# Attention mask and row minimum in one VectorE instruction per score bank, in a fused attention + MoE + MoE kernel

## The chip, the cores and the metric

The kernel runs on one core of one Trainium2 chip. The metric is device time in microseconds (us), the median of three runs; lower is better. The profile is of one further execution of the same program.

## The reference

Inputs are q, k, v of shape (4 batches, 8 heads, 576 tokens, 64), a forget factor f per head and token, and the weights of two gated MoE layers (512 to 1536 and back), all in 32-bit floats. What is computed, cut to what matters:

```python
scores = scale * np.matmul(q, k.transpose(0, 1, 3, 2))        # scale = 1/8
decay  = cum[:, :, :, None] - cum[:, :, None, :]              # cum = cumsum(log(clip(f)))
scores = np.where(causal, -1000000000.0, scores + decay)      # causal: keys after the query
scores = scores - np.max(scores, axis=-1, keepdims=True)
attn = np.exp(scores)
attn = attn / (np.sum(attn, axis=-1, keepdims=True) + 1e-09)
x = np.matmul(attn, v)                                        # then tokens x 512
x = moe_ref(rms_norm(x) * g)                                  # silu(x @ wg) * (x @ wv) @ wo
return moe2_ref(x)                                            # the same without the norm
```

## The kernel before, in words

**Stages.** The 2304 tokens are cut into four groups. Groups 0 and 1 hold the first 256 tokens of two batches each, groups 2 and 3 the other 320 tokens of two batches each. For each group the attention of its 16 heads is computed, then an RMS norm, then both MoE layers. The attention of group g+1 runs beside the MoE layers of group g, which are long rows of TensorE (PE) matmuls of 128x512 (lines 1774 to 1776: three matmuls per product, since every 32-bit operand is split into a high and a low half, called `hi` and `lo`).

**The part that the diff touches** is the attention of groups 2 and 3 ("longer blocks": up to 576 keys per query), in `pair_wide` and `wide_part`. One unit is a pair of heads; there are 2 groups x 2 batches x 4 pairs = 16 units, each with three parts. Parts 0 and 1 take 128 queries each against 384 and 512 keys, one PSUM bank per head. Part 2, the joint part, takes the last 64 queries of both heads together against 576 keys, in two banks of 288 keys. For each part:

- PE computes the scores, a `hi` and a `lo` matmul per head and bank (lines 813, 814), and adds the causal mask with one more matmul of a triangular tile `mir` (line 820, 128 columns, once per bank of parts 0 and 1; line 818, 64 columns, once per joint part).
- VectorE (DVE) takes each bank's row maximum (line 831); in the joint part it merges the two banks' maxima (line 836); it multiplies by -0.125 (line 838).
- ScalarE (ACT) computes exp(0.125 x score + bias) with the sum of the row (line 849), into the SBUF tiles `dA`, `dB`, `dC` of parts 0, 1 and 2.
- DVE merges the two sums of the joint part (line 860), adds 1e-9 (line 862), takes the reciprocal (line 863); GpSimd (POOL), ACT or DVE scales the tile by it (lines 870 to 874).
- PE transposes the tile in pieces of 128x128 (line 922 in `turn`); ACT or DVE and then DVE split the result into `ph` and `pl` (lines 310, 312, 934); PE multiplies with the values (line 950).

**What sets the order.** All work is written as Python generators, and a planner (`Plan.run`) gives each engine its list of instructions while the program is built. Each step carries a cost (`pe(n)`, `dve(n)`, ...), and the planner always issues the step that can start first by these costs, with priorities among steps that start close together. Where a step may run on several engines, it picks the one that is done first. Nothing is reordered on the chip: each engine works through its list and waits on semaphores. So any change of a cost shifts the order on all engines from the first changed step on. A unit's tiles and banks come from pools (`Take`): two parts may be scored at once, and eight PSUM banks serve everything.

**The switch.** `switch` closes the tiles of the first two groups' attention and opens those of groups 2 and 3 in the same SBUF space; there POOL clears parts of the key and query tiles (lines 422 to 426), which have to wait until the old tiles' last readers are done.

Of the kernel before, what the change touches and what calls it, by code (L numbers as in the profile page):

```python
# [27 lines left out]
LOWEST = -3.0e38  # L28
# [39 lines left out]
S_PRIO = 4.25  # L68
S_AT = (60, 2)
# [165 lines left out]
def pe(n):  # L235
    return max(0.107, n / 2400 + 0.0135)


def dve(n):
    return n / 960 + 0.152  # L240
# [40 lines left out]
def tile_attention_moe_moe(  # L281
# [57 lines left out]
    mir = sb.tile([P, 4, P], F32R, name="mir")  # L339
# [16 lines left out]
    nc.vector.tensor_copy(mir[:, 3].rearrange("p (a n) -> p a n", a=2), mask[:, :D].unsqueeze(1).to_broadcast([P, 2, D]))  # L356
# [46 lines left out]
    qk_all = []  # L403

# [380 lines left out]
    def wide_part(hds, part, st, hl, ev, e0):  # L785
# [15 lines left out]
        for groups in plan_:  # L801
            bank, eb = yield Take(banks, ())

            def mm():
                for heads, k0, m, col in groups:
                    o = bank[:, col : col + m]
                    first = True
                    for x in heads:
                        k1, kb, q1, qb = hds[x].kq
                        qs = slice(320 - D * x, 448 - D * x) if joint else slice(q0, q0 + P)  # L810
                        ks = slice(k0, k0 + m)
                        last = k0 + m < kn and x == heads[-1]
                        nc.tensor.matmul(o, q1[:, qs], k1[:, ks], start=first, stop=False)  # L813
                        nc.tensor.matmul(o, qb[:, qs], kb[:, ks], start=False, stop=last)  # L814
                        first = False
                    if k0 + m == kn:
                        if joint:
                            nc.tensor.matmul(o[:, m - D :], mir[:, 3], mir[:, 1, :D], start=False, stop=True)
                        else:
                            nc.tensor.matmul(bank[:, col + kn - P : col + kn], mir[:, 0], mir[:, 1], start=False, stop=True)  # L820

            cost = sum(2 * len(h) * pe(m) for h, _, m, _ in groups) + pe(P)
# [4 lines left out]
        c = 8 * part  # L827
        for i, (bank, e) in enumerate(zip(sc, es)):
            if kind:
                m = plan_[i][0][2]  # L830
                em = yield op("DVE", dve(m), lambda: nc.vector.tensor_reduce(st[:, c + i : c + i + 1], bank[:, :m], axis=AX.X, op=ALU.max), e)  # L831
            else:
                v = bank[:, : 2 * kn].rearrange("p (a n) -> p a n", a=2)
                em = yield op("DVE", dve(2 * kn), lambda: nc.vector.tensor_reduce(st[:, c : c + 2].unsqueeze(2), v, axis=AX.X, op=ALU.max), e)
        if joint:
            em = yield op("DVE", dve(1), lambda: nc.vector.tensor_tensor(st[:, c : c + 1], st[:, c : c + 1], st[:, c + 1 : c + 2], op=ALU.max), em)
        k = 1 if joint else 2
        em = yield op("DVE", dve(k), lambda: nc.vector.tensor_scalar(st[:, c + 2 : c + 2 + k], st[:, c : c + k], -0.125, None, op0=ALU.mult), em)
        dt, e1 = yield Take(s[("dA", "dB", "dC")[part]], ())
        ex = []  # L840
        for i in range(2):
            if joint:
                o, src, b = dt[:, JOINT * i : JOINT * (i + 1)], sc[i][:, :JOINT], 0
            else:
# [5 lines left out]
                    o, src, AF.Exp, scale=0.125, bias=st[:, c + 2 + b : c + 3 + b], accum_out=st[:, c + 4 + i : c + 5 + i]  # L850
                ), em, e1,
# [6 lines left out]
        e = ex[1]  # L858
        if joint:
            e = yield op("DVE", dve(1), lambda: nc.vector.tensor_tensor(st[:, c + 4 : c + 5], st[:, c + 4 : c + 5], st[:, c + 5 : c + 6], op=ALU.add), e)  # L860
        r = st[:, c + 4 : c + 4 + k]
        e = yield op("DVE", dve(k), lambda: nc.vector.tensor_scalar(r, r, 1e-9, None, op0=ALU.add), e)
# [749 lines left out]
    def switch():  # L1612
# [10 lines left out]
        lp = late.enter_context(tc.tile_pool(name="lp", bufs=1))  # L1623
        attention_tiles(lp, 2, LATE)
# [396 lines left out]
```

## Time and profile before

| | |
|---|---|
| three runs | 1066.35, 1068.9, 1077.26 us; median 1068.9 us |
| profiled execution | 1067.34 us, of which the span from the first to the last instruction is 1065.5 us |
| granted TensorE clock | 1.00 of full speed on average |
| PE busy | 1054.7 us (99% of the span), 5585 matmuls |
| DVE busy | 781.3 us (73%) |
| ACT busy | 602.0 us (56%) |
| POOL busy | 455.7 us (43%) |
| DMA | 76.8% of the 16 DMA engines' time |

How to read it: busy time is the union of an engine's instructions. Matmuls overlap in the PE, so the duration of one (0.39 us for 512 columns) is longer than the distance from its start to the next one's start; what a matmul costs a busy PE is that distance. The attention of groups 2 and 3 lies between 304 and 763 us; from 761 us to the end PE has MoE work alone.

### The profile page before, as it was taken

What the parts mean: (1) busy time and instruction counts of PE and PEld (TensorE: products, weight loads), DVE (VectorE), ACT (ScalarE), POOL (GpSimd) and SP (SyncE); (2) the same over time, 40 slices, a digit from 0 to 9 for tenths busy, and PEclk for the clock granted to TensorE, in tenths of its full rate; (3) what the DMA queues carried; (4) which work ended last, traced back from release to release, by engine and by line L of the source; (5) the groups of instructions that cost most, each with busy time, mean ns of one, the idle gap of its engine ahead of it and who ended that gap; (6) DMA issues with size and microseconds to landing.
All of it is one profiled execution on the core that took longest, in us unless ns stands there. A gap on an engine that the chain in (4) does not pass through costs nothing. (4 is left out here: it accounts for less than half of the span.)

```text
span 1065.5 us, 17657 instructions
## 1 busy us (share of the span) xinstructions
PE 1054.7 (99%) x5585; PEld 934.9 (88%) x5585; DVE 781.3 (73%) x1632; ACT 602.0 (56%) x1322; POOL 455.7 (43%) x490
## 2 busy tenths in 40 slices
PE   8999999999999999999999999999999999999998
PEld 8988888888888888888888888888889999999998
DVE  5888888888476647666747775877877878788773
ACT  6886768775567557657326564556643325533352
POOL 1323202214367656667325675668713340244310
PEclk9999999999999999999999999999999999999999
DMA  7766798775997786775999899998895458655583
GB/s 201 226 223 227 258 354 287 244 245 172 351 371 262 254 267 207 259 269 173 344 366 368 301 341 376 363 348 292 296 365 185 170 195 257 221 185 179 190 260 103
DMA packets 136497, 281.21 MB, mean 264 GB/s; under 512 B 14674, under 2 KB 57490, under 8 KB 136402
## 3 DMA queue, kind: packets, MB, share of 16 engines
q1 hardware_dynamic: 136404, 280.09, 76.8%
q8 instruction: 44, 0.72, 0.3%
q14 instruction: 49, 0.40, 0.1%
HBM read 193.31 MB, written 86.65 MB: 263 GB/s over the span
## 5 line engine op out<-in xcount | busy, mean ns | idle before, releaser
L315 POOL TENSOR_TENSOR whl<-w,whl 128x512 fp32r<-128x512 f32 x120 | 158.0, 1324 | 191.4 <-ACT whl L310 129.6
L1774 PE MATMUL bank<-X,whl 128*128 128x512 f32 x564 | 227.7, 404 | 0.0
L1775 PE MATMUL bank<-X,whl 128*128 128x512 f32 x564 | 220.5, 391 | 0.0
L1776 PE MATMUL bank<-X,whl 128*128 128x512 f32 x564 | 220.1, 390 | 0.0
L310 ACT CAST whl<-w 128x512 fp32r<-128x512 f32 x173 | 106.0, 618 | 38.1 <-PE bank L1775 9.3
L1776 PEld LDWEIGHTS bank<-X,whl 128*128 128x128 f32 x564 | 106.0, 188 | 23.2
L1774 PEld LDWEIGHTS bank<-X,whl 128*128 128x128 f32 x564 | 106.1, 188 | 19.8
L1775 PEld LDWEIGHTS bank<-X,whl 128*128 128x128 f32 x564 | 106.2, 188 | 18.8 <-POOL X L315 0.2
L1774 PE MATMUL bank<-H,whl 128*128 128x512 f32 x211 | 84.6, 401 | 0.0
L1775 PE MATMUL bank<-H,whl 128*128 128x512 f32 x211 | 83.2, 394 | 0.0
L1776 PE MATMUL bank<-H,whl 128*128 128x512 f32 x211 | 83.0, 393 | 0.0
L1916 ACT ACTIVATE tmp<-bank 128x384 f32<-128x384 f32 x48 | 23.5, 492 | 86.8 <-DVE bank L1515 86.2
L1929 DVE SCALAR_TENSOR_TENSOR bank<-tmp,bank 128x512 f32<-128x512 f32 x60 | 41.7, 695 | 37.9 <-PE bank L1776 37.4
L1906 ACT ACTIVATE tmp<-bank 128x512 f32<-128x512 f32 x72 | 43.1, 599 | 43.2 <-PE bank L1776 42.8
L1908 DVE SCALAR_TENSOR_TENSOR tmp<-tmp,bank 128x512 f32<-128x512 f32 x72 | 49.2, 684 | 23.9 <-ACT tmp L1906 23.5
L315 DVE TENSOR_TENSOR whl<-w,whl 128x512 fp32r<-128x512 f32 x75 | 52.8, 710 | 16.9 <-ACT whl L310 16.6
L831 DVE TENSOR_REDUCE tm<-bank 128x1 f32<-128x384 f32 (+2 forms) x96 | 51.7, 561 | 8.9 <-PE bank L814 4.8
L1702 POOL TENSOR_SCALAR w<-w,rebase 128x512 f32<-128x512 f32 x22 | 18.8, 854 | 90.7 <-DMA w<-w 55.6
L934 DVE TENSOR_TENSOR pl<-bank,ph 128x512 fp32r<-128x512 f32 (+1 forms) x80 | 49.6, 631 | 7.1 <-ACT ph L310 6.4
L1719 DVE SCALAR_TENSOR_TENSOR w<-w,wk 128x512 int32<-128x512 int32 x72 | 53.7, 753 | 0.1
L1708 ACT ACTIVATE wk<-w,kbias 128x512 uint16<-128x512 uint16 x57 | 49.9, 883 | 0.4 <-DVE w L1719 0.4
L1478 PE MATMUL bank<-X,whl 128*128 128x384 f32 x150 | 50.1, 334 | 0.0
(304 smaller groups left out, 2813.7 us busy)
## 6 DMA issues: line engine op xcount, KB each, us to landing
whl<-w_split SPq DMA_DIRECT2D x89, 512.0 KB
w<-w SPq DMA_DIRECT2D x72, 512.0 KB
w<-w_f SPq DMA_DIRECT2D x144, 256.0 KB
w_split<-whl SPq DMA_DIRECT2D x72, 512.0 KB
w_f<-w SPq DMA_DIRECT2D x72, 256.0 KB
w_sums<-w SPq DMA_DIRECT2D x48, 256.0 KB
w_sums_split<-whl SPq DMA_DIRECT2D x24, 512.0 KB
w<-w_sums SPq DMA_DIRECT2D x41, 256.0 KB
```

What stands on the lines that cost most here:

```text
L310: nc.scalar.copy(o, i)
L315: (nc.vector if e == "DVE" else nc.gpsimd).tensor_tensor(o, a, b, op=ALU.subtract)
L831: em = yield op("DVE", dve(m), lambda: nc.vector.tensor_reduce(st[:, c + i : c + i + 1], bank[:, :m], axis=AX.X, op=ALU.max), e)
L934: e = yield op("DVE", dve(n), lambda: nc.vector.tensor_tensor(low, src, o.bitcast(F32), op=ALU.subtract), e)
L1478: nc.tensor.matmul(o, w[:, 0, cs], xl, start=False, stop=False)
L1708: lambda e: nc.scalar.activation(k16[:, :, 0], x16[:, :, 1], AF.Identity, scale=1.0 / 8192, bias=kbias)
L1719: lambda: nc.vector.scalar_tensor_tensor(ti, ti, 3, k, op0=ALU.logical_shift_left, op1=ALU.bitwise_or), e, et,
L1774: nc.tensor.matmul(o, wh[:, cs], xh, start=start, stop=False)
L1775: nc.tensor.matmul(o, wh[:, cs], xl, start=False, stop=False)
L1776: nc.tensor.matmul(o, wl[:, cs], xh, start=False, stop=stop)
L1906: e = yield op("ACT", actp(n), lambda: nc.scalar.activation(a, b, AF.Tanh, scale=0.5), e, e0)
L1908: "DVE", dve(n), lambda: nc.vector.scalar_tensor_tensor(a, a, 1.0, b, op0=ALU.add, op1=ALU.mult), e,
```

## The change

In `wide_part` the mask matmuls go (lines 818 and 820, and the 64-column copy of the mask in `mir`). Two SBUF tiles in the new pool hold the mask as zeros and -2^33: `whole`, 512 columns with the triangle in the last 128, and `joint`, 288 columns with a 64-column triangle at the end. In place of maximum, merge and multiplication stands one `tensor_tensor_reduce` per bank: it reads the bank and the mask, writes -0.125 x (bank + mask) back into the bank, and gives the minimum of the row. The second instruction of the joint part starts its minimum from the first one's result. The exponentials then use scale -1, and in the joint part one instruction adds both sums and 1e-9. To the planner the new instruction costs `dve(m) + TTR`, with TTR = 0.06 us. `mask_tiles` builds the two tiles at the switch, with two memsets and two selects on POOL and one small copy on DVE.

```diff
+TTR = 0.06
...
-    nc.vector.tensor_copy(mir[:, 3].rearrange("p (a n) -> p a n", a=2), mask[:, :D].unsqueeze(1).to_broadcast([P, 2, D]))
...
+    masks = {}
+
+    def mask_tiles(pool):
+        whole, joint = (pool.tile([P, n], F32, name=f"mask{n}") for n in (KN[1] - D, JOINT))
+        nc.gpsimd.memset(whole, 0.0)
+        nc.gpsimd.memset(joint, 0.0)
+        for t, rows, n in ((whole, P, P), (joint, D, D)):
+            x = t[:rows, t.shape[1] - n :]
+            nc.gpsimd.affine_select(
+                x, x, pattern=[[-1, n]], compare_op=ALU.is_ge, fill=-BIG, base=0, channel_multiplier=1
+            )
+        nc.vector.tensor_copy(joint[D:, JOINT - D :], joint[:D, JOINT - D :])
+        masks.update(whole=whole, joint=joint)
...
-                        last = k0 + m < kn and x == heads[-1]
+                        last = x == heads[-1]
...
-                    if k0 + m == kn:
-                        if joint:
-                            nc.tensor.matmul(o[:, m - D :], mir[:, 3], mir[:, 1, :D], start=False, stop=True)
-                        else:
-                            nc.tensor.matmul(bank[:, col + kn - P : col + kn], mir[:, 0], mir[:, 1], start=False, stop=True)
-
-            cost = sum(2 * len(h) * pe(m) for h, _, m, _ in groups) + pe(P)
+
+            cost = sum(2 * len(h) * pe(m) for h, _, m, _ in groups)
...
+        low, em = [], None
         for i, (bank, e) in enumerate(zip(sc, es)):
-            if kind:
-                m = plan_[i][0][2]
-                em = yield op("DVE", dve(m), lambda: nc.vector.tensor_reduce(st[:, c + i : c + i + 1], bank[:, :m], axis=AX.X, op=ALU.max), e)
...
-        if joint:
-            em = yield op("DVE", dve(1), lambda: nc.vector.tensor_tensor(st[:, c : c + 1], st[:, c : c + 1], st[:, c + 1 : c + 2], op=ALU.max), em)
+            m = plan_[i][0][2]
+            mk = masks["joint"] if joint and i else masks["whole"][:, :m] if joint else masks["whole"][:, KN[1] - D - kn :]
+            first = st[:, c : c + 1] if joint and i else HIGHEST
+            to = st[:, c : c + 1] if joint and not i else st[:, c + 2 : c + 3] if joint else st[:, c + 2 + i : c + 3 + i]
+            em = yield op(
+                "DVE", dve(m) + TTR,
+                lambda: nc.vector.tensor_tensor_reduce(
+                    bank[:, :m], bank[:, :m], mk, -0.125, first, op0=ALU.add, op1=ALU.min, accum_out=to
+                ), e, *([em] if joint and i else []),
+            )
+            low.append(em)
         k = 1 if joint else 2
-        em = yield op("DVE", dve(k), lambda: nc.vector.tensor_scalar(st[:, c + 2 : c + 2 + k], st[:, c : c + k], -0.125, None, op0=ALU.mult), em)
...
-                    o, src, AF.Exp, scale=0.125, bias=st[:, c + 2 + b : c + 3 + b], accum_out=st[:, c + 4 + i : c + 5 + i]
-                ), em, e1,
+                    o, src, AF.Exp, scale=-1.0, bias=st[:, c + 2 + b : c + 3 + b], accum_out=st[:, c + 4 + i : c + 5 + i]
+                ), low[b if not joint else 1], e1,
...
         if joint:
-            e = yield op("DVE", dve(1), lambda: nc.vector.tensor_tensor(st[:, c + 4 : c + 5], st[:, c + 4 : c + 5], st[:, c + 5 : c + 6], op=ALU.add), e)
-        r = st[:, c + 4 : c + 4 + k]
-        e = yield op("DVE", dve(k), lambda: nc.vector.tensor_scalar(r, r, 1e-9, None, op0=ALU.add), e)
+            e = yield op("DVE", dve(1), lambda: nc.vector.scalar_tensor_tensor(r, r, 1e-9, st[:, c + 5 : c + 6], op0=ALU.add, op1=ALU.add), e)
+        else:
+            e = yield op("DVE", dve(k), lambda: nc.vector.tensor_scalar(r, r, 1e-9, None, op0=ALU.add), e)
...
         lp = late.enter_context(tc.tile_pool(name="lp", bufs=1))
+        mask_tiles(lp)
         attention_tiles(lp, 2, LATE)
```

**PE, first unit, part 1 (512 keys, both heads).** `bank` is a score bank, `k1`, `kb`, `q1`, `qb` hold keys and queries, `mir` the mask, `X` and `whl` are a MoE operand and a weight tile. Before:

```order
L813 MATMUL bank0_98<-k1_20_2491,q1_20_2493 128x512
L814 MATMUL bank0_98<-kb_20_2492,qb_20_2494 128x512
L820 MATMUL bank0_98<-mir_75 128x128
L813 MATMUL bank2_100<-k1_21_2501,q1_21_2503 128x512
L814 MATMUL bank2_100<-kb_21_2502,qb_21_2504 128x512
L820 MATMUL bank2_100<-mir_75 128x128
L1774 MATMUL bank6_104<-X1_0_114,whl0_168 128x512
```

Now:

```order
L826 MATMUL bank0_97<-k1_20_2501,q1_20_2503 128x512
L827 MATMUL bank0_97<-kb_20_2502,qb_20_2504 128x512
L826 MATMUL bank2_99<-k1_21_2511,q1_21_2513 128x512
L827 MATMUL bank2_99<-kb_21_2512,qb_21_2514 128x512
L1787 MATMUL bank6_103<-X1_0_113,whl0_167 128x512
```

The two mask matmuls are gone; 80 in the whole program (64 of 128 columns, 16 of 64), and with them 80 weight loads. Nothing stands in their place. The transpositions move as well: in this first unit, between the last score of the joint part and the first transposition of `dA`, `dB` and `dC`, there stand 2, 6 and 11 groups of three MoE matmuls before, and 2, 4 and 8 now.

**DVE, first unit, end of part 1 and the joint part.** `tm` holds the small numbers per row, `mask` is the new tile. Before:

```order
L838 TENSOR_SCALAR tm_2520<-tm_2520 128x2
L831 TENSOR_REDUCE tm_2520<-bank_100 128x1
L838 TENSOR_SCALAR tm_2520<-tm_2520 128x2
L1929 SCALAR_TENSOR_TENSOR bank_104<-tmp_69,bank_104 128x512
L862 TENSOR_SCALAR tm_2520<-tm_2520 128x2
L312 CAST whl_168<-w_5_167 128x512
L863 RECIPROCAL tm_2520<-tm_2520 128x2
L831 TENSOR_REDUCE tm_2520<-bank_102 128x1
L315 TENSOR_TENSOR H_1_131<-bank_104,H_0_130 128x512
L831 TENSOR_REDUCE tm_2520<-bank_101 128x1
L836 TENSOR_TENSOR tm_2520<-tm_2520 128x1
L838 TENSOR_SCALAR tm_2520<-tm_2520 128x1
```

Now:

```order
L844 ISA bank_99,tm_2530<-bank_99,mask_2490 128x512
L844 ISA tm_2530 128x1
L874 TENSOR_SCALAR tm_2530<-tm_2530 128x2
L1942 SCALAR_TENSOR_TENSOR bank_103<-tmp_69,bank_103 128x512
L875 RECIPROCAL tm_2530<-tm_2530 128x2
L844 ISA bank_101,tm_2530<-bank_101,mask_2490 128x288
L844 ISA tm_2530 128x1
L874 TENSOR_SCALAR tm_2530<-tm_2530 128x2
L844 ISA bank_100,tm_2530<-bank_100,mask_2491,tm_2530 128x288
L844 ISA tm_2530 128x1
```

Each new instruction is built as two: the pass over the bank, and a second one that writes the accumulated minimum into `tm`. In all, 96 maxima, 48 multiplications, 16 merges and 16 small additions go, and 96 such pairs come; the joint part's line 860 stays as one instruction on line 872.

**DVE at the switch.** Now:

```order
L1726 TENSOR_SCALAR wk_179<-w_3_184 128x512
L1732 SCALAR_TENSOR_TENSOR w_5_166<-w_5_166,wk_179 128x512
L415 COPY mask_2491<-mask_2491 64x64
L316 TENSOR_TENSOR whl_170<-w_4_165,whl_170 128x512
L316 TENSOR_TENSOR whl_172<-w_0_161,whl_172 128x512
```

Before, the same rows stand there without the copy. The copy waits for POOL's memsets and selects, and the weight splits (`whl`) stand behind it. On POOL the four new instructions stand ahead of the twelve memsets of the key and query tiles.

## Rows read from the trace of the kernel before

**Rows 1.** The page: span, then each engine's busy us, share, instructions.

```profile
span 1065.5 us, 17657 instructions
PE 1054.7 (99%) x5585; PEld 934.9 (88%) x5585; DVE 781.3 (73%) x1632; ACT 602.0 (56%) x1322; POOL 455.7 (43%) x490
```

**Rows 2.** Windows: length; busy PE, PEld, DVE, ACT, POOL; granted clock; DMA share; GB/s.

```profile
550.00:600.00 50.00, 49.71 (x251) 41.96 (x250) 35.24 (x78) 25.91 (x65) 24.76 (x35) 1.00 0.99 358
```

**Rows 3.** Waits of PE, 300 to 761 us: whom for; total us, times, longest.

```profile
PE bank L922 <- POOL dA L872: 1.8, 3, 0.9
PE bank L922 <- ACT dA L870: 0.6, 1, 0.6
PE bank L922 <- POOL dB L872: 0.6, 1, 0.6
```

**Rows 4.** Timeline of PE, first unit, parts 0 and 1: start us, duration us, instruction.

```profile
304.35 0.33 PE L813 MATMUL bank<-k,q 128*128 128x384 f32 x1
...
304.69 0.22 PE L820 MATMUL bank<-mir 128*128 128x128 f32 x1
304.76 0.39 PE L813 MATMUL bank<-k,q 128*128 128x384 f32 x1
304.99 0.35 PE L814 MATMUL bank<-kb,qb 68*128 68x384 f32 x1
...
306.39 0.45 PE L1774 MATMUL bank<-X,whl 128*128 128x512 f32 x1
306.68 0.40 PE L1775 MATMUL bank<-X,whl 128*128 128x512 f32 x1
```

**Rows 5.** Timeline of PE, first unit, the joint part.

```profile
309.23 0.29 PE L813 MATMUL bank<-k,q 128*128 128x288 f32 x1
...
310.30 0.20 PE L818 MATMUL bank<-mir 128*128 128x64 f32 x1
...
310.65 0.40 PE L1775 MATMUL bank<-X,whl 128*128 128x512 f32 x1
```

**Rows 6.** Timeline of PE, unbroken 384-column matmuls: a start and the eighth after.

```profile
799.96 0.34 PE L1479 MATMUL bank<-X,whl 128*128 128x384 f32 x1
...
801.34 0.33 PE L1478 MATMUL bank<-X,xwhl 128*128 128x384 f32 x1
```

**Rows 7.** Timeline of PE, unbroken 512-column matmuls: a start and the twelfth after.

```profile
603.15 0.40 PE L1774 MATMUL bank<-X,whl 128*128 128x512 f32 x1
...
605.90 0.39 PE L1774 MATMUL bank<-X,whl 128*128 128x512 f32 x1
```

**Rows 8.** Groups of DVE, 300 to 761 us: busy us, mean ns; idle before, releaser.

```profile
L831 DVE TENSOR_REDUCE tm<-bank 128x1 f32<-128x512 f32 x32 | 21.4, 681 | 0.1
L831 DVE TENSOR_REDUCE tm<-bank 128x1 f32<-128x384 f32 x32 | 16.7, 551 | 3.2 <-PE bank L820 3.2
L831 DVE TENSOR_REDUCE tm<-bank 128x1 f32<-128x288 f32 x32 | 14.3, 451 | 5.6 <-PE bank L814 4.8
L1929 DVE SCALAR_TENSOR_TENSOR bank<-tmp,bank 128x512 f32<-128x512 f32 x43 | 29.9, 695 | 25.5 <-PE bank L1776 25.1
L838 DVE TENSOR_SCALAR tm<-tm 128x2 f32<-128x2 f32 x32 | 6.6, 205 | 0.3
```

**Rows 9.** Groups of ACT, 300 to 761 us: the accumulator reads behind part 0's exponentials.

```profile
L849 ACT ACTIVATION_READ_ACCUMULATOR dA<-bank,tm 128x1 f32 x32 | 6.2, 195 | 0.0
```

**Rows 10.** Timelines of ACT and PE, first unit: scaling `dA`, then its transpositions.

```profile
310.00 1.12 ACT L870 ACTIVATE dA<-dA,tm 128x384 f32<-128x384 f32 x2
...
311.81 0.82 PE L922 MATMUL bank<-mi,dA 128*128 128x128 f32 x6
```

**Rows 11.** The switch: timelines of POOL and DVE; group of a select at the start.

```profile
263.68 0.57 POOL L422 MEMSET kb<- 4x576 f32 x1 [5.52 <-ACT whl L310]
...
266.79 3.10 DVE L315 TENSOR_TENSOR whl<-w,whl 128x512 fp32r<-128x512 f32 x5 [2.79 <-ACT whl L310]
...
L350 POOL TENSOR_SCALAR_AFFINE_SELECT mi<-mi 128x128 f32<-128x128 f32 x1 | 0.3, 295 | 0.1
```

More of the change, by code (lines that the diff above doesn't have):

```diff
@@ L27 @@
 BIG = 2.0**33
-LOWEST = -3.0e38
+HIGHEST = 3.0e38
 QN = (SPLIT, S - SPLIT)
@@ L338, in tile_attention_moe_moe @@
     mi = sb.tile([P, 2, P], F32, name="mi")
-    mir = sb.tile([P, 4, P], F32R, name="mir")
+    mir = sb.tile([P, 3, P], F32R, name="mir")
     mask, ident = mi[:, 0], mi[:, 1]
@@ L827, in wide_part @@
         c = 8 * part
+        low, em = [], None
         for i, (bank, e) in enumerate(zip(sc, es)):
-            if kind:
-                m = plan_[i][0][2]
-                em = yield op("DVE", dve(m), lambda: nc.vector.tensor_reduce(st[:, c + i : c + i + 1], bank[:, :m], axis=AX.X, op=ALU.max), e)
-            else:
-                v = bank[:, : 2 * kn].rearrange("p (a n) -> p a n", a=2)
-                em = yield op("DVE", dve(2 * kn), lambda: nc.vector.tensor_reduce(st[:, c : c + 2].unsqueeze(2), v, axis=AX.X, op=ALU.max), e)
-        if joint:
-            em = yield op("DVE", dve(1), lambda: nc.vector.tensor_tensor(st[:, c : c + 1], st[:, c : c + 1], st[:, c + 1 : c + 2], op=ALU.max), em)
+            m = plan_[i][0][2]
[9 more added lines that the diff above has]
+            low.append(em)
         k = 1 if joint else 2
-        em = yield op("DVE", dve(k), lambda: nc.vector.tensor_scalar(st[:, c + 2 : c + 2 + k], st[:, c : c + k], -0.125, None, op0=ALU.mult), em)
         dt, e1 = yield Take(s[("dA", "dB", "dC")[part]], ())
@@ L858, in wide_part @@
         e = ex[1]
+        r = st[:, c + 4 : c + 4 + k]
         if joint:
-            e = yield op("DVE", dve(1), lambda: nc.vector.tensor_tensor(st[:, c + 4 : c + 5], st[:, c + 4 : c + 5], st[:, c + 5 : c + 6], op=ALU.add), e)
-        r = st[:, c + 4 : c + 4 + k]
-        e = yield op("DVE", dve(k), lambda: nc.vector.tensor_scalar(r, r, 1e-9, None, op0=ALU.add), e)
+            e = yield op("DVE", dve(1), lambda: nc.vector.scalar_tensor_tensor(r, r, 1e-9, st[:, c + 5 : c + 6], op0=ALU.add, op1=ALU.add), e)
+        else:
+            e = yield op("DVE", dve(k), lambda: nc.vector.tensor_scalar(r, r, 1e-9, None, op0=ALU.add), e)
         e = yield op("DVE", dve(k) + 0.01, lambda: nc.vector.reciprocal(r, r), e)
```

## The prediction, as it was put on record

> **What bounds the kernel now.** I read the page first: PE is busy 1054.7 of 1065.5 us, and no other engine is above 73% [rows 1]. A busy PE can still be waiting inside, so I looked at its waits in the stretch where the changed attention runs. From 300 to 761 us PE waits 3.0 us in all, five times, and every one is at a transposition (line 922) whose tile had not been scaled yet [rows 3]. So in these 461 us PE goes from matmul to matmul, and the end comes earlier by whatever PE has less to do, as long as no new wait appears. The granted clock is 1.00 there [rows 2], the higher of its two levels, 2.4 GHz. From 761 us on PE has only MoE work that the change does not touch, so what is won before is kept to the end.
>
> **What a mask matmul costs PE.** The reader should look at starts, not durations. In the first unit the four score groups of parts 0 and 1 and the MoE matmul behind them reach from 304.35 to the start at 306.68, 2.33 us [rows 4]. Without masks these are four matmuls of 384 columns and five of 512. An unbroken 384 takes (801.34 - 799.96) / 8 = 0.173 us from start to start [rows 6], a 512 takes (605.90 - 603.15) / 12 = 0.229 us [rows 7]. That gives 4 x 0.173 + 5 x 0.229 = 1.84 us, so four masks cost 0.49 us. The rows show why it is 0.12 us each and not 0.06: the mask's own start-to-start is 0.07 us (304.69 to 304.76), but the 384-column matmul behind it then takes 0.23 us (304.76 to 304.99) in place of 0.173. The joint part reaches from 309.23 to 310.65, 1.42 us [rows 5]; its eight score matmuls take 1.07 us (309.23 to 310.30), and one 512 would follow in 0.229, so its mask costs 0.12 us. Together 0.61 us per unit, and 16 units give **9.8 us less on PE**. The scores and everything else on PE stay as they are: 80 matmuls go and none is added.
>
> Bounds of this term: below, only the masks' own distances, 5 x 0.07 = 0.35 us per unit or 5.6 us, if what follows a score matmul of 68 rows pays the same delay without the mask; above, the 9.8 us. I take 9.8, since rows 6 and 7 are the same kind of matmul without a mask ahead of it.
>
> The Trainium skill, page "TensorE: Matmul & The Clock Gate", section "Back-to-back issue gap", gives about 81 ns per matmul of 128 columns in a real stream of weight loads and matmuls. By that figure, called an estimate, 80 masks would be worth 6.5 us and the time 1062 us. The row differs: 0.12 us here, with the delay of the following matmul.
>
> **What DVE gets and loses.** Away go 32 maxima each of 0.681, 0.551 and 0.451 us (52.4 us), 32 multiplications of 0.205 (6.6 us) [rows 8], and 48 smaller instructions that I do not price. In come 96 passes over a bank with a second operand from SBUF. The nearest row is line 1929: two operations on a bank and an SBUF tile, written back into a bank, 0.695 us for 512 columns, against 0.681 for the maximum of the same width [rows 8]. So a pass costs what the maximum cost. The accumulator read behind it has no row on DVE. Below it is nothing, hidden in the end of the pass; above I take ACT's read, 0.195 us [rows 9]. That is 0 to 18.7 us in all; I take 0.06 to 0.1, nearer to the lower end, since the read carries one column. DVE's load in the stretch therefore changes by between -7 and +12 us out of 461, from a busy share of 35.2 in 50 us [rows 2]: it does not become the bound, and I cost it at nothing.
>
> **The chain from score to transposition.** It is shorter by the multiplication and by one place in line: the first head's exponential no longer waits for the second head's maximum (0.55 us) and for the multiplication (0.2 us). The planner knows this and uses it up: in the first unit it puts `dB`'s first transposition behind 4 groups of MoE matmuls instead of 6, `dC`'s behind 8 instead of 11, at 3 x 0.229 us each. So the cushion does not grow. It was 0.69 us in the first unit: `dA` was scaled at 310.00 + 1.12 = 311.12 and turned at 311.81 [rows 10]. The planner prices the new pair at 0.06 us over the maximum. Up to 0.1 us more per pair the cushion covers the four pairs that stand in a row; I add 1 us of new waits, a third of the 3.0 us that are there, since the joint part's transpositions come closest. Between the bounds of the read (0 to 0.195) this term runs from -3 us, when the waits of now go too, to +6 us.
>
> **The switch.** POOL's first memset starts at 263.68 and takes 0.57 us for 576 columns [rows 11]. Ahead of it now stand memsets of 512 and 288 columns, no longer than 0.57 each, and two selects of at most 0.295 us [rows 11]: at most 1.7 us. DVE's copy waits for the second select, to 265.4 at the latest, and holds the weight splits behind it. But DVE stood idle for 2.79 us before 266.79, waiting for ACT [rows 11]; the one split that it did ahead of that gap (0.7 us) fits between 265.6 and 266.79. So this costs nothing; without that gap it would be a delay of 1.7 us of one weight tile. POOL's memsets end 1.7 us later, and nothing of its next work was waiting. SP's queue gets no new transfer.
>
> **The sum.** 1067.3 us (the profiled execution) - 9.8 + 1.0 = **1058.5 us**. The profiled execution is 1.6 us under the median of 1068.9, so this is 0.8% less than its own time and 1.0% less than the median. A change under 1% is what a measurement of this kernel can hardly tell from none.
>
> **Rivals.**
>
> *Waits grow at the transpositions.* For it: the planner moves them closer, and all the waits of now are of this kind. Against: five waits among 16 x 5 transposition jobs [rows 3]. If each unit waits 0.3 us more than now, half of what it saves, the time is 1057.5 + 16 x 0.3 = 1062 us. Chance 0.17.
>
> *The new instruction needs two passes' time, and the kernel becomes slower.* From the three maxima one column costs (681 - 451) / (512 - 288) = 1.03 ns [rows 8]; at half rate a pass is longer by 0.39, 0.53 or 0.30 us. The four pairs of parts 0 and 1 stand in one row on DVE, so part 1's second head is 1.84 us late, and the joint part another 0.6; less the cushion of 0.69 that is 1.15 to 1.75 us of waiting per unit, 18 to 28 us, and the time is 1076 to 1085, say 1080 us. It decides from 0.33 us per pair on, where 4 x 0.33 eats the cushion and the 0.61 us saved. Against: line 1929 streams two operands at full rate [rows 8]. Chance 0.07. The Trainium skill, page "Vector Engine (DVE) Microarchitecture Reference", section "Points that are easy to get wrong", says that a two-tensor instruction with two SBUF sources wider than bf16 runs at half rate, since no read port is left for the accumulator; here one source is in PSUM, and no row shows an accumulating DVE instruction.
>
> *The masks free less than they seem to.* With 5.6 us as above, the time is 1067.3 - 5.6 + 1 = 1062.7 us. About the same comes if DMA sets the pace in windows like that of 550 to 600 us, where its share is 0.99 [rows 2]: were half of the stretch like that, half of the saving would be lost, and the time 1063.4 us. Against the latter: PE waits for no transfer [rows 3]. Chance 0.08. The figure of the Trainium skill's page on TensorE, named above, lies on this side.
>
> *The waits of now go as well.* The small instructions between maximum and exponential are fewer, and they are the ones with stray delays (0.205 us on average for two columns [rows 8]). Then 1067.3 - 9.8 - 3.0 = 1054.5 us. Chance 0.08.
>
> That leaves 0.60 for the forecast, within 1055.5 to 1061.
>
> **How the numbers follow.** One per cent under the median is 1058.2 us. Of the forecast a little less than half lies below it (0.28 of 0.60); with the last rival faster has 0.36. Same has the rest of the forecast (0.32), the first rival (0.17) and the third (0.08): 0.57. Slower has 0.07. The range 1055 to 1064.5 holds the forecast, most of the first and third rivals and little of the others, about 0.82.
>
> **What would show it.** PE: 80 matmuls fewer, and the stretch from the first score of part 0 to the second MoE matmul behind part 1 down from 2.33 to 1.84 us. DVE: passes of about 0.69, 0.55 and 0.46 us, reads under 0.2. Waits at the transpositions: 2 to 6 us in all. The attention's end and the end of the program both come about 9 us earlier, and from there to the end nothing changes. I am wrong if the passes are longer than 0.9 us for 512 columns, if PE begins to wait for DVE at the switch, or if the matmul behind the last score of a part still starts 0.06 us late.

## The result: 1056.9 us, about 1% faster

The changed kernel takes 1056.9 us (median of 4 runs, 1055.69 to 1057.0), the kernel before 1067.62 us (4 runs, 1065.24 to 1077.26). The ratio is 0.9887, with a 95% interval of [0.9858, 0.9917]. One of the four runs of before, 1077.26 us, weighs on this: the two medians alone give 0.990, and against the 54 further runs of the kernel before that stand beside the experiments below (medians 1066.54 to 1067.37 us) it is 0.990 to 0.991. The profiled execution took 1056.92 us, so it stands for the median. The forecast was 1058.5 us, in a range of 1055 to 1064.5.

**The page after.** Span, then each engine's busy us, share and instructions, against [rows 1]:

```profile
span 1055.1 us, 17539 instructions
PE 1045.9 (99%) x5505; PEld 926.1 (88%) x5505; DVE 772.5 (73%) x1633; ACT 602.0 (57%) x1323; POOL 467.6 (44%) x508
```

PE is still the bound, with 80 matmuls fewer and a span 10.4 us shorter. DVE lost 8.8 us of work; at a share of 73% that alone says nothing of the time.

**PE in the first unit.** Timeline of the changed kernel: start, duration, instruction. The first three rows answer to [rows 4], the last two to [rows 5].

```profile
304.74 0.34 PE L826 MATMUL bank<-k,q 128*128 128x384 f32 x1
...
306.37 0.40 PE L1787 MATMUL bank<-X,whl 128*128 128x512 f32 x1
306.60 0.39 PE L1788 MATMUL bank<-X,whl 128*128 128x512 f32 x1
...
308.43 0.30 PE L826 MATMUL bank<-k,q 128*128 128x288 f32 x1
...
309.74 0.39 PE L1788 MATMUL bank<-X,whl 128*128 128x512 f32 x1
```

From the first score of part 0 to the second MoE matmul behind part 1 it is 306.60 - 304.74 = 1.86 us, where [rows 4] had 2.33. The joint part takes 1.31 us where [rows 5] had 1.42. The delay behind a mask is gone as well: 0.23 us from 306.37 to 306.60, before 0.29 from 306.39 to 306.68. So one unit is worth 0.47 + 0.11 = 0.58 us, 16 units 9.3 us. The first unit stands for the others: counted in both traces, parts 0 and 1 took 2.32 to 2.35 us in all 16 units before and take 1.86 to 1.89 us now, and the joint part took 1.42 us in the 12 units where a MoE group follows it, and takes 1.31 us in all 16 now.

**PE's waits**, 300 to 763 us (whom for; total us, times, longest), against [rows 3]:

```profile
PE bank L934 <- POOL dA L884: 1.4, 2, 0.8
PE bank L962 <- DVE ph L946: 0.3, 1, 0.3
```

They are 1.7 us in place of 3.0. So the balance is -9.3 for the matmuls, -1.3 for the waits and +0.4 because the first score came 0.4 us later (304.74 against 304.35): -10.2 us, of 10.4 measured. That 0.4 us has no wait of PE behind it, and the kernels m1 to m5 and m8 to m12 below start that unit anywhere between 303.6 and 304.3 us; m11 has the change's own order on PE and starts it at 303.72, so one execution differs from the next by as much.

**DVE in the first unit**, timeline; below it the new instruction's groups (minimum, median and maximum of the duration in ns):

```profile
305.49 0.56 DVE L844 CUSTOM_DVE_ANT_0 bank<-bank,mask 128x384 f32<-128x384 f32 x1
305.97 0.14 DVE L844 DVE_READ_ACCUMULATOR2_ANT tm<- 128x1 f32 x1
305.97 0.60 DVE L844 CUSTOM_DVE_ANT_0 bank<-bank,mask 128x384 f32<-128x384 f32 x1
306.48 0.14 DVE L844 DVE_READ_ACCUMULATOR2_ANT tm<- 128x1 f32 x1
306.48 0.73 DVE L844 CUSTOM_DVE_ANT_0 bank<-bank,mask 128x512 f32<-128x512 f32 x1
...
307.13 0.73 DVE L844 CUSTOM_DVE_ANT_0 bank<-bank,mask 128x512 f32<-128x512 f32 x1
...
307.78 0.16 DVE L874 TENSOR_SCALAR tm<-tm 128x2 f32<-128x2 f32 x1
```

```profile
L844 DVE DVE_READ_ACCUMULATOR2_ANT tm<- x96: 83/141/144, 306.0 to 744.8; 128x1 f32 x96
L844 DVE CUSTOM_DVE_ANT_0 bank<-bank,mask x80: 440/579/734, 305.5 to 743.4; 128x384 f32<-128x384 f32 x32, 128x512 f32<-128x512 f32 x32, 128x288 f32<-128x288 f32 x16
```

The read lasts 0.14 us, but it starts in the same moment as the next pass, so in a row of passes little of it is seen. It is not quite nothing: the first 384-column pass takes 0.48 us to its read (305.49 to 305.97), the second, which starts together with a read, 0.51 (305.97 to 306.48); in m11 below, where a maximum stands between two passes, it is 0.47. For 512 columns it is 0.65 us from one pass to the next (306.48 to 307.13), 0.14 us for 128 columns more, which is 1.1 ns per column where the maxima of [rows 8] took 1.03: the pass runs at full rate.

**The way from score to transposition**, first unit. Timelines of ACT, DVE, POOL and PE, in brackets the idle time before and what ended it; against [rows 10]:

```profile
306.14 0.58 ACT L860 ACTIVATE dA<-bank,tm 128x384 f32<-128x384 f32 x1 [0.78 <-DVE tm L844]
...
308.63 0.70 DVE L1942 SCALAR_TENSOR_TENSOR bank<-tmp,bank 128x512 f32<-128x512 f32 x1 [0.69 <-PE bank L1789]
309.23 0.16 DVE L875 RECIPROCAL tm<-tm 128x2 f32<-128x2 f32 x1
...
309.56 1.16 POOL L884 TENSOR_SCALAR dA<-dA,tm 128x384 f32<-128x384 f32 x2 [2.33 <-DVE tm L875]
...
310.88 0.82 PE L934 MATMUL bank<-mi,dA 128*128 128x128 f32 x6
311.45 0.48 PE L1787 MATMUL bank<-X,whl 128*128 128x512 f32 x1
```

Both exponentials of `dA` were done by 307.4 us, but the reciprocal stands on DVE behind a MoE instruction that waits for PE, and comes at 309.23. The tile was scaled at 309.56 + 1.16 = 310.72 and turned at 310.88: 0.16 us between the two, where there had been 0.69.

**The switch**, timelines of POOL and DVE, against [rows 11]:

```profile
263.99 0.53 POOL L408 MEMSET mask<- 128x512 f32 x1 [5.42 <-ACT whl L311]
...
265.28 0.57 POOL L435 MEMSET kb<- 4x576 f32 x1
...
265.26 0.65 DVE L415 COPY mask<-mask 64x64 f32<-64x64 f32 x1 [1.47 <-POOL mask L412]
...
267.18 3.10 DVE L316 TENSOR_TENSOR whl<-w,whl 128x512 fp32r<-128x512 f32 x5 [0.55 <-ACT whl L311]
```

POOL's four new instructions took 1.3 us and DVE's copy 0.65. The splits behind it started 0.4 us later than before, behind a gap of 0.55 us in which DVE waited for ACT and not for the copy, and no wait of PE stands there.

### The profile page after: what moved, and what is told of

It is laid out like the page before. It is cut to its first block, busy times and chain, and to the rows that moved or that the text cites. A ratio compares the mean times of both kernels' runs of the same rounds, so it can differ in the third digit from the quotient of the medians.

```text
span 1055.1 us, 17539 instructions
## 1 busy us (share of the span) xinstructions
PE 1045.9 (99%) x5505; PEld 926.1 (88%) x5505; DVE 772.5 (73%) x1633; ACT 602.0 (57%) x1323; POOL 467.6 (44%) x508
## 4 chain that ended last, share of the span: by engine, by line
PE 93%; POOL 2%; issue 2%; DMA 1%; DVE 1%; ACT 1%; POOLq 0%; ACTq 0%; DVEq 0%
PE bank L1787 18%; PE bank L1788 18%; PE bank L1789 18%; PE bank L1489 6%; PE bank L1490 6%; PE bank L1491 6%; PE bank L962 3%; PE bank L934 3%; PE bank L1398 3%; PE bank L1399 3%; PE bank L1397 3%; PE bank L827 2%; PE bank L826 2%; PE bank L683 2%; PE bank L736 1%
## 5 line engine op out<-in xcount | busy, mean ns | idle before, releaser
L316 POOL TENSOR_TENSOR whl<-w,whl 128x512 fp32r<-128x512 f32 x123 | 162.4, 1326 | 206.3 <-ACT whl L311 153.1
L311 ACT CAST whl<-w 128x512 fp32r<-128x512 f32 x180 | 109.9, 618 | 40.0 <-PE bank L1788 13.1
L1787 PE MATMUL bank<-H,whl 128*128 128x512 f32 x208 | 83.3, 401 | 0.0
L1788 PE MATMUL bank<-H,whl 128*128 128x512 f32 x208 | 82.1, 395 | 0.0
L1789 PE MATMUL bank<-H,whl 128*128 128x512 f32 x208 | 81.7, 393 | 0.0
L1942 DVE SCALAR_TENSOR_TENSOR bank<-tmp,bank 128x512 f32<-128x512 f32 x60 | 41.7, 695 | 35.2 <-PE bank L1789 34.7
L844 DVE CUSTOM_DVE_ANT_0 bank<-bank,mask 128x384 f32<-128x384 f32 (+2 forms) x80 | 45.9, 609 | 12.1 <-PE bank L827 11.7
L1490 PE MATMUL bank<-X,whl 128*128 128x384 f32 x154 | 51.5, 334 | 0.0
L1489 PE MATMUL bank<-X,whl 128*128 128x384 f32 x154 | 51.5, 334 | 0.0
```

The lines of the kernel that those rows point to most:

```text
L311: nc.scalar.copy(o, i)
L316: (nc.vector if e == "DVE" else nc.gpsimd).tensor_tensor(o, a, b, op=ALU.subtract)
L844: lambda: nc.vector.tensor_tensor_reduce(bank[:, :m], bank[:, :m], mk, -0.125, first, op0=ALU.add, op1=ALU.min, accum_out=to), e, *([em] i ...
L1489: nc.tensor.matmul(o, w[:, 0, cs], xh, start=c == 0, stop=False)
L1490: nc.tensor.matmul(o, w[:, 0, cs], xl, start=False, stop=False)
L1787: nc.tensor.matmul(o, wh[:, cs], xh, start=start, stop=False)
```

## The experiments

Theory: the 9 to 10 us are PE's mask matmuls and nothing else, and what is left over, a few us in either direction, is how the planner's re-made order happens to fall at the transpositions. Rivals: DVE's shorter chain brings part of the gain, or a mask matmul is worth its own 0.07 us only. Each kernel is compared with runs of the kernel before on the same chip, whose medians were 1066.54 us (m1 to m4), 1067.37 us (m5 to m8) and 1067.22 us (m9 to m12). "Waits" are those of PE that the trace lists from 300 to 763 us, in the one profiled execution. That execution is not always a typical one: m2's and m9's were the longest of their nine and ten runs (1073.53 and 1068.67 us), m6's the shortest of its five.

| | us, median (runs) | ratio to before, 95% | waits, us |
|---|---|---|---|
| before, beside the change | 1067.62 (4) | 1 | 3.0 |
| the change | 1056.9 (4) | 0.9887 [0.9858, 0.9917] | 1.7 |
| m1 before without masks | 1056.25 (4) | 0.990 [0.9881, 0.9919] | 1.4 |
| m2 change with mask matmuls | 1070.36 (9) | 1.0036 [1.002, 1.0052] | 7.8 |
| m10 the same, price 0.30 | 1068.19 (10) | 1.0006 [0.9993, 1.002] | 3.4 |
| m12 the same, price 0.12 | 1068.15 (10) | 1.0006 [0.9992, 1.002] | 3.8 |
| m9 before, maxima priced +0.06 | 1065.99 (10) | 0.9988 [0.9975, 1.0002] | 2.9 |
| m3 before, masks twice | 1074.28 (4) | 1.0069 [1.0053, 1.0085] | 1.7 |
| m4 change, price -0.40 | 1064.55 (10) | 0.9973 [0.996, 0.9987] | 6.4 |
| m8 change, price 0.12 | 1057.64 (4) | 0.991 [0.9885, 0.9935] | 2.1 |
| m5 change, price 0.30 | 1058.01 (4) | 0.9908 [0.9888, 0.9928] | 3.4 |
| m11 change, an extra pass per bank | 1072.86 (6) | 1.0048 [1.0032, 1.0064] | 12.9 |
| m6 no mask matmul in any group | 1061.32 (5) | 0.9952 [0.9911, 0.9993] | 3.2 |
| m7 nor in group 1 | 1059.44 (5) | 0.9928 [0.9898, 0.9957] | 1.4 |

**m1: PE's part alone.** The kernel before, without the 80 mask matmuls; DVE keeps its maxima and multiplications.

```diff
-                    if k0 + m == kn:
-                        if joint:
-                            nc.tensor.matmul(o[:, m - D :], mir[:, 3], mir[:, 1, :D], start=False, stop=True)
...
-            cost = sum(2 * len(h) * pe(m) for h, _, m, _ in groups) + pe(P)
+            cost = sum(2 * len(h) * pe(m) for h, _, m, _ in groups)
```

> The kernel before without its 80 mask matmuls in groups 2 and 3, and everything on VectorE as it was (the mask of these two groups is left out of the computation). If the gain of the change is TensorE's (theory: 0.12 us per mask matmul, 0.61 us per unit), this alone gives 1067.6 - 9.8 = 1058 us, within 1.5 us of the changed kernel's 1057. If the gain came from the shorter chain on VectorE, this stays above 1064 us.

It gives the whole gain: 10.3 us, a ratio of 0.990 against the change's 0.9887, with intervals that overlap. The time is within the theory's 1.5 us of the change. DVE's rearrangement is not needed for it.

**m2, m10, m12: DVE's part alone.** The change, with the mask matmuls back on PE, at three prices of the new instruction.

```diff
-                        last = x == heads[-1]
+                        last = k0 + m < kn and x == heads[-1]
...
+                            nc.tensor.matmul(bank[:, col + kn - P : col + kn], mir[:, 0], mir[:, 1], start=False, stop=True)
...
-TTR = 0.06
+TTR = 0.3
```

> The changed kernel with the mask matmuls put back on TensorE as well, so that the mask is added twice; VectorE works as in the change. Theory: the 9.8 us are gone again, 1067 us, since VectorE's chain only moves the transpositions and the planner uses its shortening up. Rival: the shorter chain is worth something by itself, the 1 to 2 us of waits that went: 1064 to 1065 us.

> The change with the mask matmuls kept on PE (as in the earlier run that took 1070.4 us), but with the new DVE instruction priced at +0.30 us in place of +0.06. Theory (the 3 to 4 us that the earlier run lay above the kernel before were chance in the order): the waits at the transpositions fall from 8 to 2 to 4 us and the time to 1065 to 1067.5 us. Rival (mask matmuls on PE and the new DVE instruction do not go together: PE is later with each part and the planner puts the transpositions closer): waits of 6 us or more and 1069 to 1072 us at this price too.

> As the run with both masks and a price of +0.30, with +0.12 us. Theory (chance in the order): 1065 to 1069 us, with waits that need not lie between those of the prices 0.06 and 0.30. Rival (the two do not go together): 1069 to 1072 us, waits of 6 us or more.

m2 missed both expectations: it was 3.8 us slower than before. Its waits, in the same view as above:

```profile
PE bank L940 <- POOL dA L890: 6.0, 7, 1.6
PE bank L940 <- ACT dA L888: 1.4, 1, 1.4
```

The other two prices move the order and nothing else, and most of the excess goes: 3.4 and 3.8 us of waits, 1068.2 us twice, within 1 us of before (m10's theory had said 1067.5 at most). So DVE's part alone gains nothing at any of the three prices (1.0006 [0.9993, 1.002] at two of them), and m2's 3.8 us are put down to an order that fell badly. Its 7.8 us of waits are from an execution 3.2 us over its median, so they overstate what this order costs.

**m9: the order alone.** The kernel before, with one price changed.

```diff
-                em = yield op("DVE", dve(m), lambda: nc.vector.tensor_reduce(st[:, c + i : c + i + 1], bank[:, :m], axis=AX.X, op=ALU.max), e)
+                em = yield op("DVE", dve(m) + 0.06, lambda: nc.vector.tensor_reduce(st[:, c + i : c + i + 1], bank[:, :m], axis=AX.X, op=ALU.max), e)
```

> The kernel before, with each row maximum of parts 0, 1 and 2 priced 0.06 us higher to the planner; no instruction is added or removed, so PE's load is the same and only the order of the work can change. Theory (the waits at the transpositions depend on how the order happens to fall): the time moves by up to 4 us in either direction from 1067 us, and the waits of PE between 300 and 761 us come out anywhere between 1.5 and 7 us in place of 3.0. Rival (the order before was a good one, and any other price for DVE's pass is worse): slower by 3 us or more. Second rival (the price does not matter): within 1 us, with 3 us of waits.

The total of the waits stayed (2.9 us), but they are others: one of 2.1 us for a sum that DVE had not finished takes the place of those for POOL and ACT.

```profile
PE bank L922 <- DVE tm L862: 2.1, 1, 2.1
```

The time, 1065.99 us, cannot be told from before. By the time alone the second rival (the price does not matter) fits; the changed waits show that the order did move, though in an execution 2.7 us over the median.

**m3: the price of a mask.** Each mask matmul issued twice.

```diff
-                            nc.tensor.matmul(bank[:, col + kn - P : col + kn], mir[:, 0], mir[:, 1], start=False, stop=True)
+                        for n in range(2):
...
+                                nc.tensor.matmul(bank[:, col + kn - P : col + kn], mir[:, 0], mir[:, 1], start=False, stop=n == 1)
```

> The kernel before with each of the 80 mask matmuls issued twice. Theory: a matmul of 128 or 64 columns costs TensorE about 0.11 to 0.12 us with what it delays behind it, so 80 more cost 9 to 10 us: 1077 us. Rival: what a mask costs is its own distance of 0.07 us, and the rest is a delay that the score matmul has anyway: 5 us more, 1073 us. A start to start of 0.06 us twice in a row would speak for the rival, one of 0.11 for the theory.

Timeline of PE, first unit, parts 0 and 1:

```profile
304.10 0.33 PE L813 MATMUL bank<-k,q 128*128 128x384 f32 x1
...
304.45 0.34 PE L821 MATMUL bank<-mir 128*128 128x128 f32 x2
304.62 0.39 PE L813 MATMUL bank<-k,q 128*128 128x384 f32 x1
...
306.59 0.44 PE L1775 MATMUL bank<-X,whl 128*128 128x512 f32 x1
```

From the first score to the first MoE matmul it is 2.49 us, in [rows 4] 2.04 us: four more masks cost 0.45 us, 0.11 each. From the first mask to the score behind both it is 0.17 us (304.45 to 304.62), where one mask took 0.07 [rows 4]: by the trace 0.06 to the second mask and 0.11 from there, so that a matmul behind a short one starts late here too. The time rose by 7.7 us, less than the theory's 9 to 10 and more than the rival's 5; the waits listed are 1.3 us fewer than before, and 7.7 + 1.3 = 9.0 us stands beside 80 x 0.11 = 8.8. So the rows decide for the theory, and the time fits it only with the waits counted in.

**m8, m5, m4: the order at other prices.** The change, with one constant changed: 0.12 in m8, 0.3 in m5, -0.4 in m4.

```diff
-TTR = 0.06
+TTR = 0.12
```

> The changed kernel with TTR = 0.12 in place of 0.06: the planner's order changes a little and nothing else. If the 1 to 2 us of waits are a matter of how the order happens to fall, this scatters within 2 us of the changed kernel, 1055 to 1059 us; if the cushion alone decides, it is between the changed kernel and the one with 0.3, within 0.5 us of them.

> The changed kernel with TTR = 0.3: the planner takes each pass and read for 0.24 us more than in the change and puts the transpositions about 1.5 us later behind the scores. If the waits at the transpositions come from a cushion that is too small, they go from 1.7 us to near 0 and the time to 1055.5 us. Rival: tiles and banks are held longer and other steps wait: 1057 us or more.

> The changed kernel with TTR = -0.4, so that the planner takes each pass and read for 0.46 us less than before: what the chip does is as in the change, but every pair is 0.46 us later than planned, as if the instruction ran at half rate. By the arithmetic of the prediction's slower rival (four pairs in a row, less a cushion of 0.69 us) this costs 1.15 us per unit, 18 us: 1075 us. Rival, from the order of TensorE's instructions: the transpositions stand only 0.5 to 0.9 us closer behind the scores than in the change, about as much as the cushion, so that the waits grow by 0 to 0.5 us per unit: 1057 to 1065 us.

A higher price should give every tile more room. In m5 it does for `dA`: counted in the trace, its first transposition stands 3.4 groups of MoE matmuls behind the unit's last score on average, in the change 1.9. Yet the waits do not go: 2.1 us in m8 and 3.4 us in m5 against the change's 1.7, and the time is 1 us longer or the same. In m8, whose time cannot tell its two expectations apart, nearly all of them are not at a transposition; PE waits for a query tile:

```profile
PE bank L826 <- POOL q L316: 1.9, 2, 1.0
```

A price that is 0.46 us lower per pair does cost: m4 takes 7.7 us over the change, 4.7 us of them in listed waits. That is at the upper end of the rival's range and far from the 18 us of the theory.

**m11: the prediction's slower rival, made to happen.** The change, with an unused row maximum ahead of each new instruction, without a price.

```diff
-                lambda: nc.vector.tensor_tensor_reduce(
+                lambda: (nc.vector.tensor_reduce(st[:, c + 6 + i : c + 7 + i], bank[:, :m], axis=AX.X, op=ALU.max), nc.vector.tensor_tensor_reduce(
```

> The change with one more row maximum on DVE ahead of each new instruction (96 of them, 0.45 to 0.68 us each, its result unused), which the planner does not know of: the order on every engine is that of the change, and each pair takes about as long as it would at half rate. The prediction's arithmetic (four pairs in a row, less a cushion of 0.69 us): 1.8 us or more of waiting per unit, 28 us in all, and 1080 to 1090 us. Rival (the four pairs do not all stand in one row, since MoE matmuls lie between the scores and the transpositions, and a late tile delays only its own transposition, as the run with the price 0.46 us too low showed with 7.7 us): 1063 to 1070 us, with 8 to 15 us of waits for dA and dB.

The time is 1072.86 us, between the two: 16 us over the change, 1.0 us per unit. Its waits (two of five rows), then timelines of DVE, POOL and PE in the first unit, which begins at 303.72 us here:

```profile
PE bank L934 <- POOL dA L884: 9.6, 13, 1.5
PE bank L934 <- ACT dA L882: 1.6, 2, 0.9
```

```profile
304.47 0.55 DVE L844 TENSOR_REDUCE tm<-bank 128x1 f32<-128x384 f32 x1
304.94 0.56 DVE L844 CUSTOM_DVE_ANT_0 bank<-bank,mask 128x384 f32<-128x384 f32 x1
305.41 0.14 DVE L844 DVE_READ_ACCUMULATOR2_ANT tm<- 128x1 f32 x1
...
308.77 0.16 DVE L874 TENSOR_SCALAR tm<-tm 128x2 f32<-128x2 f32 x1
308.84 0.69 DVE L1942 SCALAR_TENSOR_TENSOR bank<-tmp,bank 128x512 f32<-128x512 f32 x1
309.44 0.15 DVE L875 RECIPROCAL tm<-tm 128x2 f32<-128x2 f32 x1
...
309.77 1.15 POOL L884 TENSOR_SCALAR dA<-dA,tm 128x384 f32<-128x384 f32 x2 [3.56 <-ACT dB L860]
...
310.41 1.11 PE L934 MATMUL bank<-mi,dA 128*128 128x128 f32 x6 [0.40 <-POOL dA L884]
311.28 0.48 PE L1787 MATMUL bank<-X,whl 128*128 128x512 f32 x1
```

Counted from the first score, the row of four pairs ends 5.05 us in, in the change 3.04: 2.0 us late. But the reciprocal comes only 1.2 us late (5.72 against 4.49), since DVE no longer stands idle ahead of L1942, where the change had it wait 0.69 us for PE. The transposition begins 0.55 us late (6.69 against 6.14), while POOL is still scaling the second head, since its first pieces need the first head alone. The six pieces then take 1.11 us in place of 0.82, and the MoE matmul behind them starts 0.85 us late (7.56 against 6.71). So this one transposition brings most of the 1.0 us that a unit costs on average, and only 0.40 us of it are listed as a wait.

**m6 and m7: further down the same road.** The same edit in the attention of groups 0 and 1 (m6), or of group 1 alone (m7).

```diff
-                nc.tensor.matmul(
-                    bank[:, : 2 * kn].rearrange("p (a n) -> p a n", a=2)[:, :, kn - P :], mir[:, 0], mir[:, 1:3], start=False, stop=True
-                )
...
+                    low[x, c] = yield op(
+                        "DVE", dve(kn) + TTR,
+                        lambda: nc.vector.tensor_tensor_reduce(
+                            i, i, maskq[:, 2 * P - kn :], -0.125, HIGHEST, op0=ALU.add, op1=ALU.min, accum_out=to
+                        ), e, e0,
+                    )
```

> The changed kernel with the same edit in the blocks of groups 0 and 1 too: their 32 mask matmuls of 256 columns go, and 64 passes of 128 or 256 columns take the place of 32 maxima over two heads and 16 multiplications. In the trace of the changed kernel such a mask matmul takes 0.21 to 0.31 us from start to start, 0.26 on average, so if TensorE bounds both groups this gives 8 us: 1049 us. Rival: in group 0 (first 60 us) TensorE waits for others anyway, and only the 16 of group 1 count: 1053 us. Second rival: VectorE, busy 85% between 100 and 200 us, gets 32 instructions more and delays the norm or the weight splits: 1057 us or more.

> The changed kernel with the same edit in the blocks of group 1 too, group 0 as before: 16 mask matmuls of 256 columns fewer. By 0.26 us each: 4 us, 1053 us. Rival: VectorE is the tighter engine there and nothing is gained: 1057 us.

Neither beats the change. Windows of m6 (length; busy us and instructions of PE, PEld, DVE, ACT, POOL; clock; DMA share; GB/s), up to its first score of groups 2 and 3 and from there on, then the same of the change:

```profile
0.00:299.58 299.58, 296.74 (x1534) 252.50 (x1535) 237.35 (x551) 216.37 (x420) 71.67 (x91) 1.00 0.78 256
299.58:1054.40 754.82, 747.76 (x3963) 671.26 (x3961) 542.61 (x1168) 392.13 (x913) 385.25 (x403) 1.00 0.78 271
```

```profile
0.00:304.73 304.73, 300.81 (x1552) 256.20 (x1553) 236.54 (x473) 212.09 (x416) 84.88 (x108) 1.00 0.78 258
304.73:1055.10 750.37, 745.04 (x3954) 669.92 (x3952) 535.92 (x1160) 389.93 (x908) 382.71 (x401) 1.00 0.77 270
```

The longer blocks begin 5.15 us earlier, but 9 matmuls more stand behind that point (3963 against 3954), 9 x 0.229 = 2.1 us of MoE work that was only moved. So 3.1 us were won, and the stretch behind is 4.45 us longer: 2.1 for the nine, 2.4 given back. Part of this stands among the waits, 1.1 us for a query tile that POOL splits:

```profile
PE bank L827 <- POOL q L316: 1.1, 1, 1.1
```

Of the 8 us expected 3.1 came, and the trace shows where part of the rest is: in pauses that the planner foresees for PE in the first 60 us it puts idle matmuls (line 382 of the change's kernel), and m6 has 34 of them in place of 11, which from start to start take 4.4 us in place of 1.8. So some of the time that the masks left there had no other work to go to, as the first rival said. This execution was the shortest of m6's five (1056.18 to 1069.62 us); why the others are longer is open, since no trace shows them. In m7 the longer blocks begin 1.5 us later than in the change, with new waits of 0.9 us for a weight tile that DVE splits and 0.8 us for `p` in the first 300 us, and with 30 idle matmuls that take 5.4 us. So m7's rival (VectorE is the tighter engine) has 0.9 us to show for it, and in m6 a late DVE shows in no new wait of PE; the rest of why m7 lost time is open.

## Why the prediction was right, step by step

- **PE's term** (-9.8 us): 9.3 us by the first unit's rows. Right, and for the stated reason: the delay of the matmul behind a mask is part of its price, and it went with the mask. m3 gives 0.11 us per mask from the other side, m1 shows that this term alone makes the gain. The low bound (5.6 us) is out, and with it the rival that masks free less. The Trainium skill, "TensorE: Matmul & The Clock Gate", section "Back-to-back issue gap", gives about 81 ns per matmul of 128 columns in a real stream; the runs show 0.11 to 0.12 us for a mask among wider matmuls, 0.03 to 0.04 us more.
- **The DVE pass**: 0.72, 0.57 and 0.46 us (means of the groups) were measured for 0.69, 0.55 and 0.46 predicted; the joint part's second pass, which starts from the first one's result, takes 0.52. The read is 0.14 us, between the bounds, and hidden but for 0.03 to 0.04 us on a pass that starts with it. DVE stays off the bound.
- **The waits** (+1.0 us) are the step that was off: -1.3 us, toward the rival by which they go. The reason for the +1.0 was that the planner moves the transpositions closer, read from the first unit. Counted in the traces over all 16 units that does not hold where it matters: `dA`, at which 2.4 of the 3.0 us of waits stood, is first turned 1.1 groups of MoE matmuls behind the unit's last score before (in four units directly behind it) and 1.9 now; for `dB` it is 5.8 and 6.1, and only `dC` moved closer, 11.8 and 9.6. Room alone does not set the term either: m5 gives `dA` more of it without fewer waits, m2 against m12 shows 4 us more waits for 0.06 us of price (in an execution of m2 that was 3.2 us over its median), and m9 replaces most of them at no change of the kernel's work. Over the orders tried, m4 and m11 left out, the waits run from 1.4 to 7.8 us, each read from one execution. Such a term has a size of some us and, before the run, no sign.
- **The switch** at nothing: right, with a copy that took longer (0.65 us) than thought.
- **The sum**: 1058.5 against 1056.9 us, 1.6 too high: 2.3 too high in the waits, less 0.5 in PE's term and 0.4 in the start of the longer blocks. So the sum came closer than its worst term by luck, since the misses lie in opposite directions. The attention's last matmul came 11 us earlier and the stretch behind it grew by 0.8 us; the prediction had 9 and 0. The same kernel work is split elsewhere: m9 has that matmul 10 us later than before and ends at the same time, so the place is no sign of anything. The end itself was misread: the last attention matmul of the kernel before starts at 768.3 us, not by 761 or 763; as no wait of PE lies behind 761, nothing hangs on it.
- **The slower rival** was priced too high. For m11's extra 0.47, 0.60 and 0.36 us (starts of the maximum to those of the pass) its arithmetic gives 2 x 0.47 + 2 x 0.60 - 0.69 = 1.45 us per unit without the joint part and, with 2 x 0.36 for it, 2.2 us: 23 to 35 us; 16 us came. Two things were missing in it: DVE's idle time inside the chain takes up part of the delay (2.0 us late become 1.2), and a transposition can start on one head's tile, so the cushion is not the 0.69 us of [rows 10] alone. At half rate (0.39, 0.53 and 0.30 us) the same proportion gives 1070 us, an estimate, not 1080. The rule of the Trainium skill, "Vector Engine (DVE) Microarchitecture Reference", section "Points that are easy to get wrong", on two SBUF sources remains untested: here one source is a bank, and 512 columns took 0.65 us from start to start.
- **The chances** leaned to "within 1%" (0.57); the ratio came at 1.1%, just past that border, with an interval that holds both, and by the medians it is 1.0% or a little less. The side is decided by the one run of 1077.26 us. The forecast lay at the border too.

Open: which of the planner's choices makes an order fall well, and how much of a difference in waits is the order's and how much the execution's, since each kernel was profiled once. The listed waits do not hold all that a late tile costs: m11 has 11.2 us more of them, and from the first score on 16.2 us more time. In its first unit the difference is the delay inside the row of transpositions.

## What to carry to other kernels

Where one engine runs without gaps, price a removed instruction by the starts around it: from the last start ahead of it to the second start behind it, since the neighbour's delay goes too. Where a planner re-makes the order, any edit shifts waits by a few us in either direction; try two or three neighbouring prices before reading a difference of that size as the edit's own. And price a late step only after following it to the waiting engine, since idle time on the way takes part of it up.

## What the runs showed of the hardware

DVE's accumulator read (0.14 us) overlaps the next pass, which takes 0.51 us in place of 0.47 to 0.48 for 384 columns, as the rows of the first unit and of m11 show. A DVE instruction on one column can last over a microsecond. Here is a merge of two sums (two SBUF inputs) without a POOL instruction beside it, then one with POOL's split beside it, and the merge's group:

```profile
313.29 0.15 DVE L872 SCALAR_TENSOR_TENSOR tm<-tm 128x1 f32<-128x1 f32 x1
...
363.81 1.42 POOL L316 TENSOR_TENSOR kb<-raw,k 64x576 fp32r<-64x576 f32 x1
363.93 1.32 DVE L872 SCALAR_TENSOR_TENSOR tm<-tm 128x1 f32<-128x1 f32 x1
```

```profile
L872 DVE SCALAR_TENSOR_TENSOR tm<-tm x16: 148/446/1321, 313.3 to 747.8; 128x1 f32<-128x1 f32 x16
```

The second started 0.12 us after POOL's instruction and ended with it (365.25 and 365.23). In the change's trace 12 of the 16 merges take over 0.19 us, and each of them ends within 0.02 us of the end of a POOL instruction that started before it; the other four take 0.15 to 0.17 us. The Trainium skill, "SBUF — State Buffer", section "SBUF: two separate sides", says that a DVE instruction with two SBUF inputs and a POOL instruction that reads SBUF share a pair of ports, which the one that starts first holds for its whole length; these rows agree. The new pass reads one SBUF tile, and its 96 durations (440 to 734 ns) show no such wait.
